# A recorded program and a list scheduler in the kernel, in place of the framework's scheduler, for the second half of an attention, MLP and token-mixer kernel

## The chip, the cores and the metric

The kernel runs on one core of a Trainium2 chip. A core has five engines that each work through their own instructions in order: TensorE (PE, matrix products into PSUM banks), ScalarE (ACT), VectorE (DVE), GpSimd (POOL), and SyncE (SP), which here issues the DMA transfers. They wait for each other by semaphores. The metric is the device time of one execution in microseconds, as the median of the runs.

## The reference

Three layers follow each other, with two batches of 768 tokens and a width of 512.

```python
def _attn_ref(q, k, v):            # 8 heads of 64
    k_sum = k.reshape(B, H, nb, block, D).max(axis=3)      # blocks of 32 tokens
    v_sum = v.reshape(B, H, nb, block, D).mean(axis=3)
    # scores: |i - j| < 16 locally, and q . k_sum + log(32) for each block
    a = softmax(concat(scores_local, scores_blocks))
    return a @ concat(v, v_sum)

def _moe_ref(x, g_ln, w_ch1, w_ch2):
    xn = (x - mu) / np.sqrt(var + 1e-06) * g_ln
    return x + np.maximum(xn @ w_ch1, 0.0) @ w_ch2         # 512 -> 2048 -> 512

def _moe2_ref(x, w_theta, w_tok_r, w_tok_i, w_ch):
    theta = x @ w_theta
    zr, zi = x * np.cos(theta), x * np.sin(theta)
    y = w_tok_r @ zr + w_tok_i @ zi                        # over the 768 tokens
    u = x + y
    return u + np.maximum(u @ w_ch, 0.0)
```

## The kernel before, in words

The 12 tiles of 128 tokens (x_b_t, six for each batch) pass through attention and are gathered in three chunks of four tiles for the MLP. A float32 factor is held as a high and a low float16 half (suffix h and l, or the indices 0 and 1), and a product is three float16 products. For each of the 16 blocks f of the hidden width a chunk does `up` (12 products of 512 columns, L489), `relu` on ACT into the high half h (L493), `relu_low` on DVE for the low half (L497), and `down` (12 products, L508) into four PSUM banks; `add` (L513) puts these onto x. In the program strings the words U, i, j, X and Y are up, relu, relu_low, down and add, numbered 0 to 47 over the three chunks: U32 to U47 are chunk 2, the third.

The mixer has three parts. `rest(t)` (L539 to L561) makes theta of one tile with 12 products, then sine and cosine (L542 to L548), the rotated halves and their sums (L549 to L557), and splits each into a high half (ACT, L560) and a low half (POOL, L561); tiles come to it turned (`turn`, L877 to L879: cast on ACT, difference on POOL, DMA transpose). The token product is done in seven products m1 to m7 for each batch and half (`mix`, L595, 18 products of 384 columns each) with sums and differences of the token weights (b11, t1, t2, b21, t3, b22, t4). Their results are added into u (L603 on DVE, L606 on POOL; `whole_x`, L579 on POOL, starts u from x), and a finished u is split again into x2 (L615 on ACT, L616 on DVE). `channel` (L676) is the last product, with its result at L681 to L685.

Weights come as raw words; head (ACT, L140), whole (DVE, L146), high (ACT, L153) and low (POOL, L156) convert them. The token weights are converted tile by tile during chunks 1 and 2 (`token_jobs`, DVE differences at L196, splits at L186 on ACT and L187 on POOL). Three of their seven blocks, t3, b22 and t4 (SPILLED), do not fit beside the MLP: they are stored to HBM (L793) and read back at L707 when the MLP's space is free.

What sets the order: PE runs in program order throughout. Up to the middle of chunk 1 all engines follow START, an order written out by hand. Behind that, from U24 on (SECOND, then chunk 2's `steps`, then `run_end`), the framework's scheduler chooses the order of ACT, DVE, POOL and SP, with `tc.high_priority()` around the relus and the mixer's results. The token jobs are handed out between steps at fixed rates (`advance`). The framework may also put instructions of the second half into START's holes; it does so with five L140, three L146, one L877 and four loads.

Of the kernel before, what the change touches and what calls it, by code (L numbers as in the profile page):

```python
# [22 lines left out]
P = 128  # L23
NT = S // P
# [64 lines left out]

@with_exitstack  # L90
def attention_mlp_mixer(ctx: ExitStack, tc: tile.TileContext, qd, kw, vt, vp, g_ln, w1, w2, wth, wtr, wti, wch,
                        c_mask_l, c_mask_r, c_ident, out):
    nc = tc.nc
# [13 lines left out]

    def piece(name):

        return pieces.tile([P, 512], F16, tag="piece", name=name, bufs=4 * NF)  # L110
# [302 lines left out]
    class Chunk:  # L413
# [69 lines left out]
        def up(self, f):  # L483
            xh, xl = self.x[:, 0:KT, :], self.x[:, KT:, :]
            ph = self.ph[f] = banks.take()
            wh, wl = (w.rearrange("p (k n) -> p k n", k=KT) for w in w1_s[f])
            terms = [(wh, z, k) for k in range(KT) for z in (xh, xl)] + [(wl, xh, k) for k in range(KT)]
            for n, (a, z, k) in enumerate(terms):
                nc.tensor.matmul(ph, a[:, k, :], z[:, k, :], start=(n == 0), stop=(n == len(terms) - 1))  # L489

# [9 lines left out]
        def down(self, f):  # L500
            if f == 0:
                self.pc = [banks.take() for i in range(4)]
            h = self.h.pop(f)
            hh, hl = h[:, 0, :], h[:, 1, :]
            wh, wl = w2_s[f]
            for i in range(4):
                for n, (a, z) in enumerate(((hh, wh), (hh, wl), (hl, wh))):
                    nc.tensor.matmul(self.pc[i], a[:, i * P:(i + 1) * P], z, start=(f == 0 and n == 0), stop=(f == NF - 1 and n == 2))  # L508
            hls.give(h)

# [5 lines left out]
        def steps(self, first=0):  # L516

            def step(n):
                f = n // 2
                if n % 2 == 0 and f < NF:  # L520
                    self.up(f)
                    with tc.high_priority():
                        self.relu(f)
                        self.relu_low(f)
                if n % 2 and f >= 2:
                    self.down(f - 2)
                if n == 2 * NF + 3:
# [53 lines left out]
    def mix(b, g):  # L581
# [5 lines left out]
        def product(name):  # L587
            key, part, block = PRODUCTS[name]
            bank[name] = banks.take()
            col = (part + g) * P  # L590
            w = blocks[block]
            for t in range(NT):
                z = zs[b, t][key]
                for n, (a, e) in enumerate(((0, 0), (0, 1), (1, 0))):
                    nc.tensor.matmul(bank[name][:, 0:CH], z[a][:, col:col + P], w[:, e, t, :],  # L595
                                     start=(t == 0 and n == 0), stop=(t == NT - 1 and n == 2))

        def onto(name, what, into):
            with tc.high_priority():
                onto_now(name, what, into)  # L600

        def onto_now(name, what, into):
            nc.vector.scalar_tensor_tensor(out=into, in0=bank[name][:, 0:CH], scalar=1.0 / WS, in1=what, op0=ALU.mult, op1=ALU.add)  # L603
# [7 lines left out]
        def result(name, d, c):  # L611
            u, xh, xl = us[b, d, c], x2[b, c][:, d, :], x2[b, c][:, KT + d, :]
            onto(name, u, u)
            with tc.high_priority():
                nc.scalar.copy(xh, u)  # L615
                nc.vector.tensor_tensor(out=xl, in0=u, in1=xh, op=ALU.subtract)  # L616

        def m1():
            product("m1")
            left["s"] = temps.take()  # L620
            with tc.high_priority():
                nc.scalar.mul(left["s"], bank["m1"][:, 0:CH], 1.0 / WS)
            banks.give(bank["m1"])
            plus(lo, 0, "s")
# [75 lines left out]
    def run_end(turn, rest):  # L700
# [3 lines left out]
        for t in range(2):  # L704
            turn(t)
        for name in SPILLED:
            nc.sync.dma_start(out=blocks[name], in_=spilled[name])  # L707
# [3 lines left out]
        turn(2)  # L711
# [86 lines left out]
    def attention_done():  # L798
# [3 lines left out]
        late = ctx.enter_context(tc.tile_pool(name="late", bufs=1, side="right"))  # L802
# [24 lines left out]
    def run(program):  # L827
# [5 lines left out]

        def urgent(name):
            def step(f):
                with tc.high_priority():
                    mlp_step(name)(f)
            return step

# [15 lines left out]
            "U": mlp_step("up"), "i": urgent("relu"), "j": urgent("relu_low"), "X": mlp_step("down"),  # L855
# [47 lines left out]

    for name in run(SECOND):
        if name in "UX":
            advance(SECOND_RATE)
    spare = mlp.tile([P, 2 * KT, MC], F16, tag="x", name="xt", bufs=2).rearrange("p a b -> p (a b)").bitcast(F32)
# [25 lines left out]
    run_end(*rotate(1, free, free))  # L933

# [56 lines left out]
```

## Time and profile before

| | |
|---|---|
| runs, us | 498.72, 502.1, 503.67; median 502.1 |
| profiled execution, us | 500.46 (span 498.7) |
| mean granted TensorE clock | 0.983 |
| PE busy | 471.3 us, 95% of the span |
| DVE, ACT, POOL busy | 300.7, 224.1, 227.8 us |
| DMA | 61.69 MB, mean 124 GB/s |

The span is what the trace covers, from the first to the last record; the profiled execution's own time is 1.8 us longer. The granted clock is a share of 2.4 GHz, the upper of the two levels; the lower, 1.2 GHz, reads 0.50. In the rows a line such as L497 is a line of the kernel, `ps` is a PSUM bank, and square brackets name the idle time of the engine before the row and what ended it.

### The profile page before, as it was taken

The page shows a single profiled execution, that of the slowest core. Times are in us where ns is not written, and L with a number is a line of the kernel's source. Part 1 is how long each engine was busy: PE and PEld are TensorE (multiplying, and loading weights), DVE is VectorE, ACT ScalarE, POOL GpSimd, SP SyncE. Part 2 cuts the span into 40 slices and gives each one's busy share as a digit, 9 for nine tenths or more (in the row PEclk, how much of TensorE's full clock was granted, in tenths as well). Part 3 has the DMA queues.
Part 4 walks back from the last instruction along what each step waited for, and adds up shares of the span by engine and source line. Part 5 has one row for each costly group of instructions (what it writes and reads, how often), then busy time and mean ns, then how long its engine had stood idle before and what let it go on. Part 6 is the DMA issues. An engine that isn't in the chain of part 4 may idle for free. (4 is left out here: it accounts for less than half of the span.)

```text
span 498.7 us, 8654 instructions
## 1 busy us (share of the span) xinstructions
PE 471.3 (95%) x3360; PEld 245.5 (49%) x3360; DVE 300.7 (60%) x480; ACT 224.1 (45%) x469; POOL 227.8 (46%) x254
## 2 busy tenths in 40 slices
PE   7899999999999999799989979999999995999997
PEld 2567765455544444244434424444555552556664
DVE  4388989999841211831497865665707687934332
ACT  1359896736751111640375565554504435422022
POOL 3747035746000000940397755666595755890200
PEclk9999999999999999999999989999999997999999
DMA  8989969786753000560277680000095100110012
GB/s 300 301 285 272 240 200 284 228 207 190 245 187 63 1 0 1 143 171 14 63 212 227 188 251 2 0 1 1 0 327 64 22 1 2 62 34 17 0 48 95
DMA packets 51401, 61.69 MB, mean 124 GB/s; under 512 B 23478, under 2 KB 38720, under 8 KB 50976
## 3 DMA queue, kind: packets, MB, share of 16 engines
q1 hardware_dynamic: 51072, 60.62, 42.4%
q8 instruction: 26, 0.43, 0.4%
q10 hardware_dynamic: 288, 0.52, 0.4%
q14 instruction: 15, 0.12, 0.1%
HBM read 48.80 MB, written 6.68 MB: 111 GB/s over the span
## 5 line engine op out<-in xcount | busy, mean ns | idle before, releaser
L508 PE MATMUL ps<-w,h 128*128 128x512 f16 x576 | 131.5, 382 | 6.0 <-DVE h L497 3.5
L489 PE MATMUL ps<-xt,w 128*128 128x512 f16 x576 | 129.3, 379 | 0.0
L508 PEld LDWEIGHTS <-h 128*128 128x128 f16 x576 | 56.0, 99 | 75.9 <-DVE h L497 5.4
L489 PEld LDWEIGHTS <-w 128*128 128x128 f16 x576 | 56.0, 98 | 66.8
L497 DVE SCALAR_TENSOR_TENSOR h<-ps,h 128x512 f16<-128x512 f32 x48 | 32.9, 685 | 62.5 <-ACT h L493 62.3
L493 ACT ACTIVATE h<-ps 128x512 f16<-128x512 f32 x48 | 28.5, 593 | 61.2 <-PE ps L489 51.1
L146 DVE SCALAR_TENSOR_TENSOR w<-raw,hd 128x512 int32<-128x512 int32 (+1 forms) x55 | 45.3, 832 | 12.0 <-ACT hd L140 4.5
L140 ACT ACTIVATE hd<-raw 128x512 f16<-128x512 bf16 (+1 forms) x64 | 45.8, 727 | 9.7 <-DMA raw<-in_w 3.2
L156 POOL TENSOR_TENSOR w<-w,w 128x512 f16<-128x512 f32 x20 | 27.1, 1358 | 37.7 <-ACT w L153 22.5
L676 PE MATMUL ps<-x,ch 128*128 128x384 f16 (+1 forms) x204 | 34.7, 331 | 5.7 <-ACT x L615 5.5
L539 PE MATMUL ps<-th,x 128*128 128x512 f16 x144 | 34.8, 394 | 3.7 <-DVE h L497 3.7
L676 PEld LDWEIGHTS <-ch 128*128 128x128 f16 x204 | 20.2, 101 | 19.5 <-issue 7.8
L878 POOL TENSOR_TENSOR xhl<-x,xhl 128x512 f16<-128x512 f32 x6 | 7.8, 1313 | 45.9 <-ACT xhl L877 45.9
L304 POOL TENSOR_TENSOR raw<-raw 128x384 f32<-128x384 f32 (+3 forms) x32 | 19.4, 607 | 17.8 <-DMA raw<-in_vt 15.9
L352 ACT ACTIVATE pr<-ps,nb 128x120 f32<-128x120 f32 x96 | 26.6, 366 | 0.7
L539 PEld LDWEIGHTS <-x 128*128 128x128 f16 x144 | 14.6, 101 | 21.7 <-issue 6.5
L595 PE MATMUL ps<-tok_t,z_s12h 128*128 128x384 f16 x96 | 23.4, 326 | 0.0
L261 PE MATMUL ps<-idle 128*128 128x512 bf16 x60 | 21.5, 435 | 1.0 <-DVE idle L766 1.0
L156 POOL TENSOR_TENSOR th<-w,th 128x512 f16<-128x512 f32 x4 | 5.1, 1270 | 35.2 <-ACT th L153 35.2
L342 DVE TENSOR_REDUCE nm<-ps 128x4 f32<-128x480 f32 x24 | 14.8, 649 | 10.1 <-PE ps L403 10.1
L187 POOL TENSOR_TENSOR xt<-w,xt 128x384 f16<-128x384 f32 x8 | 8.5, 1065 | 25.9 <-ACT xt L186 25.9
L403 PE MATMUL ps<-k,qt 64*64 64x96 f32 x384 | 15.9, 263 | 3.5 <-issue 2.2
(168 smaller groups left out, 798.9 us busy)
## 6 DMA issues: line engine op xcount, KB each, us to landing
raw<-in_w SPq DMA_DIRECT2D x16, 511.8 KB, 4.5
raw<-in_w SPq DMA_DIRECT2D x16, 511.0 KB, 5.0
vw<-in_vp SPq DMA_DIRECT2D x12, 396.0 KB, 7.3
raw<-in_wtr SPq DMA_DIRECT2D x12, 383.8 KB, 3.7
raw<-in_wti SPq DMA_DIRECT2D x12, 383.8 KB, 3.7
k<-in_kw SPq DMA_DIRECT2D x8, 400.0 KB, 8.8
raw<-in_vt SPq DMA_DIRECT2D x8, 384.0 KB, 7.6
qt<-in_qd SPq DMA_DIRECT2D x10, 256.0 KB, 5.4
```

Source lines behind the costliest of these rows:

```text
L140: nc.scalar.mul(out, st["raw"].bitcast(BF16)[:, 0:4 * k * n].rearrange("p (x w) -> p x w", w=4)[:, :, 2], HEAD_SCALE)
L146: nc.vector.scalar_tensor_tensor(out=st["w"].bitcast(I32), in0=rest, scalar=13, in1=st["head"].bitcast(I32)[:, 0:k * n], op0=ALU.logical_s ...
L156: engine.tensor_tensor(out=lo(), in0=st["w"], in1=st["h"], op=ALU.subtract)
L261: nc.tensor.matmul(bank.rearrange("p (r n) -> p r n", n=P), idle, idle.unsqueeze(1).to_broadcast([P, 4, P]), start=True, stop=True)
L352: nc.scalar.activation(out=self.pr[:, h, :], in_=self.sc[:, h, :], func=AF.Exp, bias=self.nb[:, h:h + 1], scale=SCALE)
L489: nc.tensor.matmul(ph, a[:, k, :], z[:, k, :], start=(n == 0), stop=(n == len(terms) - 1))
L493: nc.scalar.activation(out=self.h[f][:, 0, :], in_=self.ph[f], func=AF.Relu)
L497: nc.vector.scalar_tensor_tensor(out=h[:, 1, :], in0=self.ph[f], scalar=0.0, in1=h[:, 0, :], op0=ALU.max, op1=ALU.subtract)
L508: nc.tensor.matmul(self.pc[i], a[:, i * P:(i + 1) * P], z, start=(f == 0 and n == 0), stop=(f == NF - 1 and n == 2))
L539: nc.tensor.matmul(pt, xt[:, a, o:o + P], w[:, k, :], start=(n == 0), stop=(n == 3 * KT - 1))
L595: nc.tensor.matmul(bank[name][:, 0:CH], z[a][:, col:col + P], w[:, e, t, :], start=(t == 0 and n == 0), stop=(t == NT - 1 and n == 2))
L676: nc.tensor.matmul(pos[e][:, lo:hi], w[:, e * P:(e + 1) * P], z[:, a, lo:hi], start=(k == ORDER[0] and i == 0), stop=(k == ORDER[-1] and i ...
```

## The change

A class `Plan` stands between the kernel and the engines. Between `nc.begin()` and `nc.emit()` it records each instruction instead of issuing it, with what it reads and writes and a cost for its engine. `emit` then issues all of them in an order of its own: PE keeps its program order, which gives each PE instruction a time; from these a `due` time is worked out backwards for everything that feeds PE; and a list scheduler takes, of the instructions that can start within 0.1 us of the earliest one, the one that is due first. There are two such records: from U24 to the end of chunk 2, and `run_end`. Both are issued under `tc.manual_schedule()`, so the framework keeps this order and puts nothing of it into START. `high_priority` is gone. The 64 half-weight tiles (`pieces`) are now an explicit ring that `up`, `down` and `product` give back to. `turn(2)` stands ahead of the reload, each reload is recorded `behind` the SP instruction before it, and the reloaded blocks' places in the `end` pool come before x2's.

```diff
+class Plan:
+    ENGINES = {"tensor": "PE", "scalar": "ACT", "vector": "DVE", "gpsimd": "POOL", "sync": "SP"}
+    PATIENCE = 0.1
...
+        if op.engine == "SP":
+            op.landing = math.prod(out.shape) * mybir.dt.size(out.dtype) / 2.5e5
...
+    def behind(self):
+        n = len(self.ops)
+        yield
+        for op in self.ops[n:]:
+            op.before.add(next(x for x in reversed(self.ops[:n]) if x.engine == op.engine))
...
+    def cost(self, engine, out, ins):
+        n = math.prod(out.shape[1:])
+        psum = any(a.space == PSUM for a in ins)
+        wide = sum(a.space != PSUM and math.prod(a.shape[1:]) == n for a in ins)
+        if engine == "PE":
+            return (math.prod(ins[1].shape[1:]) / 2.4 + 5) / 1e3
+        if engine == "ACT":
+            return (190 + 0.82 * n) / 1e3 if n > 8 else 0.2
+        if engine == "DVE":
+            if n <= 8:
+                return 0.18 if not ins or math.prod(ins[0].shape[1:]) <= 8 else 0.69
+            return (150 + n * (1.04 if psum or wide > 1 else 0.65) * (1.25 if wide > 1 else 1.0)) / 1e3
+        if engine == "POOL":
+            return (200 + 2.2 * n) / 1e3 if n > 8 else 0.6
+        return 0.42
...
+    def emit(self):
+        ops, self.ops = self.ops, None
...
+        at = self.free["PE"]
+        for op in ops:
+            op.due = math.inf
+            if op.engine == "PE":
+                op.due = at
+                at += op.cost
+        for op in reversed(ops):
+            for other in op.after:
+                op.due = min(op.due, other.due - self.lag(op, other) - op.cost)
+            if op.due == math.inf:
+                op.due = at
...
+            op = min((x for x in ready[e] if max(self.free[e], x.when) <= first + self.PATIENCE), key=lambda x: (x.due, x.n))
...
-    nc = tc.nc
+    nc = Plan(tc.nc)
...
-        return pieces.tile([P, 512], F16, tag="piece", name=name, bufs=4 * NF)
+        return slots.take()
...
-                    with tc.high_priority():
-                        self.relu(f)
-                        self.relu_low(f)
+                    self.relu(f)
+                    self.relu_low(f)
...
-        for t in range(2):
+        for t in range(3):
             turn(t)
         for name in SPILLED:
-            nc.sync.dma_start(out=blocks[name], in_=spilled[name])
+            with nc.behind():
+                nc.sync.dma_start(out=blocks[name], in_=spilled[name])
         whole_x(0)
         m1, m6, m5, m2, m7, m3, m4 = mixes[0, 0]
         m1()
-        turn(2)
...
+    nc.begin()
     for name in run(SECOND):
...
+    with tc.manual_schedule():
+        nc.emit()
...
+    for name in reversed(SPILLED):
+        blocks[name] = end.tile([P, 2, NT, CH], F16, name=f"tok_{name}")
     for c in range(2):
         x2[1, c] = end.tile([P, 2 * KT, CH], F16, name=f"x2_1_{c}")
-    for name in SPILLED:
-        blocks[name] = end.tile([P, 2, NT, CH], F16, name=f"tok_{name}")
...
+    nc.begin()
     run_end(*rotate(1, free, free))
+    with tc.manual_schedule():
+        nc.emit()
```

PE's instructions stand in the same order in both kernels. Recorded instructions all have the line L111 in the new kernel, those of START L108. First ACT, where START ends. Before, the relu of f = 23 (the L493 row with ps3) stands behind three conversions of w_theta and the cast L445 that needs rstd:

```order
L153 CAST th0_2252<-w1_101 128x512
L153 CAST th0_2252<-w2_102 128x512
L153 CAST th0_2252<-w0_100 128x512
L445 ACTIVATE xhl0_107<-xn0_105,rstd_2266 128x512
L493 ACTIVATE h2_111<-ps3_66 128x512
```

Now it stands first:

```order
L111 ACTIVATE h2_175<-ps3_66 128x512
L111 CAST xhl1_172<-x_0_0_75 128x512
L111 ACTIVATE xhl0_171<-xn0_169,rstd_2264 128x512
L111 ACTIVATE h0_173<-ps7_70 128x512
L111 ACTIVATE hd0_167<-raw0_160 128x512
```

The relu of f = 23 moved ahead of the cast with rstd, the next relu (h0 from ps7) stands right behind that cast, and the conversions follow.

Next DVE in the token work, from the last two `add` of chunk 1 to relu_low of chunk 2's f = 0 (the row with h2 and ps7). Before (xt is the space of x of chunk 1, used for token words):

```order
L513 SCALAR_TENSOR_TENSOR x_1_0_81<-ps6_69,x_1_0_81 128x512
L196 TENSOR_TENSOR xt_2573<-xt_2573,w2_102 128x384
L513 SCALAR_TENSOR_TENSOR x_1_1_82<-ps5_68,x_1_1_82 128x512
L196 TENSOR_TENSOR w1_101<-w1_101,xt_2573 128x384
L146 SCALAR_TENSOR_TENSOR xt_2573<-raw3_99,hd1_104 128x384
L146 SCALAR_TENSOR_TENSOR w2_102<-raw2_98,hd0_103 128x384
L196 TENSOR_TENSOR w0_100<-xt_2573,w0_100 128x384
L146 SCALAR_TENSOR_TENSOR xt_2573<-raw1_97,hd1_104 128x384
L196 TENSOR_TENSOR xt_2573<-w2_102,xt_2573 128x384
L497 SCALAR_TENSOR_TENSOR h2_111<-ps7_70,h2_111 128x512
```

Now:

```order
L111 SCALAR_TENSOR_TENSOR x_1_0_81<-ps6_69,x_1_0_81 128x512
L111 SCALAR_TENSOR_TENSOR x_1_1_82<-ps5_68,x_1_1_82 128x512
L111 TENSOR_TENSOR xt_1515<-xt_1515,w2_166 128x384
L111 SCALAR_TENSOR_TENSOR xt_1515<-raw3_163,hd1_168 128x384
L111 TENSOR_TENSOR w1_165<-w1_165,xt_1515 128x384
L111 SCALAR_TENSOR_TENSOR w2_166<-raw2_162,hd0_167 128x384
L111 SCALAR_TENSOR_TENSOR xt_1515<-raw1_161,hd1_168 128x384
L111 SCALAR_TENSOR_TENSOR h2_175<-ps7_70,h2_175 128x512
L111 TENSOR_TENSOR w0_164<-xt_1515,w0_164 128x384
```

Two token differences (w0 and xt) moved behind the relu_low. Up to relu_low of f = 5 there are 30 DVE instructions before and 23 now.

Then DVE at the start of `run_end`. Before, u_0_1 and u_2_1 (L603, which add a product's bank onto u) stand ahead of rest(0) of the second batch, whose first three rows work in x_0_4 and x_0_5:

```order
L603 SCALAR_TENSOR_TENSOR tp1_3436<-ps6_69,tp0_3435 128x384
L603 SCALAR_TENSOR_TENSOR u_0_1_3428<-ps7_70,u_0_1_3428 128x384
L603 SCALAR_TENSOR_TENSOR u_2_1_3432<-ps7_70,u_2_1_3432 128x384
L542 TENSOR_SCALAR x_0_4_79<-ps4_67 128x512
L543 TENSOR_SCALAR x_0_4_79<-x_0_4_79 128x512
L544 SCALAR_TENSOR_TENSOR x_0_5_80<-ps4_67,x_0_4_79 128x512
```

Now:

```order
L111 SCALAR_TENSOR_TENSOR tp1_3388<-ps6_69,tp0_3387 128x384
L111 TENSOR_SCALAR x_0_4_79<-ps4_67 128x512
L111 TENSOR_SCALAR x_0_4_79<-x_0_4_79 128x512
L111 SCALAR_TENSOR_TENSOR x_0_5_80<-ps4_67,x_0_4_79 128x512
L111 SCALAR_TENSOR_TENSOR u_0_1_3380<-ps7_70,u_0_1_3380 128x384
L111 SCALAR_TENSOR_TENSOR u_2_1_3384<-ps7_70,u_2_1_3384 128x384
```

The three rows of rest(0) moved ahead of the two that need POOL's sums in u. On POOL, whole_x is no longer one block of eight: the order there is whole_x of u_0_0, its sum, whole_x of u_0_1 and u_2_1, their sums, and so on.

Last SP at the reload. Before:

```order
L879 DMA_TRANSPOSE x2_1_0_3422<-x_0_0_75 128x8x128
L879 DMA_TRANSPOSE x2_1_0_3422<-x_0_1_76 128x8x128
L707 DMA tok_t3_3424<-spilled_t3_171 128x4608
L707 DMA tok_b22_3425<-spilled_b22_172 128x4608
L707 DMA tok_t4_3426<-spilled_t4_173 128x4608
L879 DMA_TRANSPOSE x2_1_0_3422<-x_0_2_77 128x8x128
```

Now:

```order
L111 DMA_TRANSPOSE x2_1_0_3377<-x_0_0_75 128x8x128
L111 DMA_TRANSPOSE x2_1_0_3377<-x_0_2_77 128x8x128
L111 DMA_TRANSPOSE x2_1_0_3377<-x_0_1_76 128x8x128
L111 DMA tok_t3_3376<-spilled_t3_235 128x4608
L111 DMA tok_b22_3375<-spilled_b22_236 128x4608
L111 DMA_TRANSPOSE x2_1_1_3378<-x_0_3_78 128x8x128
L111 DMA_TRANSPOSE x2_1_1_3378<-x_0_0_75 128x8x128
L111 DMA tok_t4_3374<-spilled_t4_237 128x4608
```

A third transpose moved ahead of the reloads, and two more stand between b22's reload and t4's.

## Rows read from the trace of the kernel before

**Rows 1.** PE timeline: start, busy us, engine, line, operation [idle before <-releaser]

```profile
198.25 5.35 PE L489 MATMUL ps<-xt,w 128*128 128x512 f16 x24
...
220.84 2.75 PE L489 MATMUL ps<-xt,w 128*128 128x512 f16 x12
```

**Rows 2.** ACT timeline where START ends

```profile
203.65 0.72 ACT L445 ACTIVATE xhl<-xn,rstd 128x512 f16<-128x512 f32 x1 [2.90 <-POOL rstd L434]
```

**Rows 3.** PE timeline, end of chunk 1 and token work

```profile
249.33 7.93 PE L489 MATMUL ps<-xt,w 128*128 128x512 f16 x36
...
260.10 3.86 PE L508 MATMUL ps<-w,h 128*128 128x512 f16 x10 [1.04 <-DVE h L497]
263.79 2.75 PE L489 MATMUL ps<-xt,w 128*128 128x512 f16 x12
266.38 2.75 PE L508 MATMUL ps<-w,h 128*128 128x512 f16 x12
...
287.10 2.75 PE L489 MATMUL ps<-xt,w 128*128 128x512 f16 x12
293.52 4.44 PE L539 MATMUL ps<-th,x 128*128 128x512 f16 x12 [3.66 <-DVE h L497]
297.79 2.75 PE L508 MATMUL ps<-w,h 128*128 128x512 f16 x12
```

**Rows 4.** PE timeline, end stage

```profile
380.09 0.49 PE L595 MATMUL ps<-tok_t,z_ih 128*128 128x384 f16 x2
...
411.26 1.63 PE L676 MATMUL ps<-x,ch 128*128 128x384 f16 x9
418.39 0.48 PE L676 MATMUL ps<-x,ch 128*128 128x384 f16 x1 [5.50 <-ACT x L615]
...
423.54 2.81 PE L539 MATMUL ps<-th,x 128*128 128x512 f16 x12
426.19 7.96 PE L676 MATMUL ps<-x,ch 128*128 128x384 f16 x48
433.99 2.93 PE L595 MATMUL ps<-tok_b,z_r 128*128 128x384 f16 x17
437.44 0.34 PE L595 MATMUL ps<-tok_b,z_r 128*128 128x384 f16 x1 [0.52 <-POOL z_r L561]
```

**Rows 5.** Windows: stretch, busy us of five engines, clock, DMA share, GB/s

```profile
260.00:263.80 3.80, 3.70 (x11) 1.39 (x12) 2.99 (x5) 2.61 (x6) 3.80 (x5) 0.58 0.60 181
...
297.80:408.60 110.80, 110.80 (x577) 56.35 (x576) 66.09 (x103) 48.88 (x90) 70.01 (x69) 1.00 0.19 50
418.40:423.50 5.10, 4.86 (x15) 2.12 (x15) 3.84 (x7) 2.71 (x5) 2.96 (x3) 0.50 0.00 0
```

**Rows 6.** DVE timeline, then POOL timeline, token work

```profile
257.24 0.55 DVE L196 TENSOR_TENSOR w<-xt,w 128x384 f32<-128x384 f32 x1
...
258.18 1.26 DVE L196 TENSOR_TENSOR xt<-w,xt 128x384 f32<-128x384 f32 x1
...
261.43 1.25 DVE L196 TENSOR_TENSOR xt<-xt,w 128x384 f32<-128x384 f32 x1 [0.81 <-POOL tok_b L187]
...
257.98 1.04 POOL L187 TENSOR_TENSOR xt<-w,xt 128x384 f16<-128x384 f32 x1 [1.08 <-ACT xt L186]
```

**Rows 7.** DVE timeline, then POOL timeline, end stage

```profile
375.00 0.56 DVE L603 SCALAR_TENSOR_TENSOR u<-ps,u 128x384 f32<-128x384 f32 x1 [10.96 <-POOL u L606]
...
400.61 0.68 DVE L542 TENSOR_SCALAR tr<-ps 128x512 f32<-128x512 f32 x1
...
418.37 0.68 DVE L616 TENSOR_TENSOR x<-u,x 128x384 f16<-128x384 f32 x1 [0.74 <-ACT x L615]
...
364.96 6.99 POOL L579 TENSOR_TENSOR u<-x 128x384 f32<-128x384 f16 x8
```

**Rows 8.** SP timeline, reload

```profile
364.42 0.38 SPq L707 DMA_DIRECT2D tok_t<-spilled_t  x1
```

**Rows 9.** DMA issues, 355 to 400 us: KB each, us to landing

```profile
tok_b<-spilled_b SPq DMA_DIRECT2D x1, 1152.0 KB, 9.0
```

More of the change, by code (lines that the diff above doesn't have):

```diff
@@ L1 @@
 import math
-from contextlib import ExitStack
+from contextlib import ExitStack, contextmanager
 import numpy as np
@@ L90, in attention_mlp_mixer, with __init__, __getattr__ @@
+class Planned:
+    def __init__(self, plan, name):
+        self.plan, self.name = plan, name
+    def __getattr__(self, method):
+        return lambda *args, **kwargs: self.plan.call(self.name, method, args, kwargs)
+class Op:
+    def __init__(self, n, engine, do):
+        self.n, self.engine, self.do, self.before, self.landing = n, engine, do, set(), 0.0
 @with_exitstack
@@ L106, in attention_mlp_mixer @@
     pieces = ctx.enter_context(tc.tile_pool(name="pieces", bufs=1))
+    slots = Ring(*(pieces.tile([P, 512], F16, name=f"pc{i}") for i in range(4 * NF)))
+    slot_of = {x.tensor.name: x for x in slots.free}
     def piece(name):
-        return pieces.tile([P, 512], F16, tag="piece", name=name, bufs=4 * NF)
+        return slots.take()
     mlp_cm = tc.tile_pool(name="mlp", bufs=1)
@@ L489, in up @@
                 nc.tensor.matmul(ph, a[:, k, :], z[:, k, :], start=(n == 0), stop=(n == len(terms) - 1))
+            if self is chunks[-1]:
+                for x in w1_s[f]:
+                    slots.give(x)
         def relu(self, f):
@@ L509, in down @@
             hls.give(h)
+            if self is chunks[-1]:
+                for x in w2_s[f]:
+                    slots.give(x)
         def add(self, i):
@@ L588, in product @@
             key, part, block = PRODUCTS[name]
+            last = (name, g) in (("m1", 1), ("m5", 1), ("m3", 1), ("m4", 1))
             bank[name] = banks.take()
@@ L596, in product @@
                                      start=(t == 0 and n == 0), stop=(t == NT - 1 and n == 2))
+                if last and b == 0:
+                    for x in ({z[0].tensor.name: z[0].tensor, z[1].tensor.name: z[1].tensor}).values():
+                        slots.give(slot_of[x.name])
         def onto(name, what, into):
-            with tc.high_priority():
-                onto_now(name, what, into)
-        def onto_now(name, what, into):
             nc.vector.scalar_tensor_tensor(out=into, in0=bank[name][:, 0:CH], scalar=1.0 / WS, in1=what, op0=ALU.mult, op1=ALU.add)
@@ L613, in result @@
             onto(name, u, u)
-            with tc.high_priority():
-                nc.scalar.copy(xh, u)
-                nc.vector.tensor_tensor(out=xl, in0=u, in1=xh, op=ALU.subtract)
+            nc.scalar.copy(xh, u)
+            nc.vector.tensor_tensor(out=xl, in0=u, in1=xh, op=ALU.subtract)
         def m1():
@@ L620, in m1 @@
             left["s"] = temps.take()
-            with tc.high_priority():
-                nc.scalar.mul(left["s"], bank["m1"][:, 0:CH], 1.0 / WS)
+            nc.scalar.mul(left["s"], bank["m1"][:, 0:CH], 1.0 / WS)
             banks.give(bank["m1"])
@@ L801, in attention_done @@
         at_cm.__exit__(None, None, None)
-        late = ctx.enter_context(tc.tile_pool(name="late", bufs=1, side="right"))
+        late = ctx.enter_context(tc.tile_pool(name="late", bufs=1, side="right", reuse_waits="tile"))
         th.extend(late.tile([P, KT, DM], F16, name=f"th{n}") for n in range(2))
@@ L832, in run @@
         job = lambda n, *a: lambda i: w_jobs[i][n](*a)
[L834 to L838, printed above, removed]
         does = {
@@ L854, in run @@
             "dg": chunk("scale"), "fl": chunk("flip"), "fh": chunk("flipped_high"), "fz": chunk("flipped_low"),
-            "U": mlp_step("up"), "i": urgent("relu"), "j": urgent("relu_low"), "X": mlp_step("down"),
+            "U": mlp_step("up"), "i": mlp_step("relu"), "j": mlp_step("relu_low"), "X": mlp_step("down"),
             "l": job(0), "A": job(1), "D": job(2), "H": job(3), "I": job(4),
@@ L906, in attention_mlp_mixer @@
             advance(SECOND_RATE)
-    spare = mlp.tile([P, 2 * KT, MC], F16, tag="x", name="xt", bufs=2).rearrange("p a b -> p (a b)").bitcast(F32)
+    spare = chunks[1].x.rearrange("p a b -> p (a b)").bitcast(F32)
     stages = Ring(*(spare[:, i * CH:(i + 1) * CH] for i in range(3)))
```

88 lines of the change are left out of this document (added).

## The prediction, as it was made before the changed kernel ran

> **What bounds the kernel now.** I read the line of matrix-engine (PE) starts first, since PE is 95% busy and the change leaves PE's own instruction order as it was; the time can only come from PE's gaps. Twelve 512-column products are one step: 263.79 to 266.38 is 2.59 us [rows 3]; a 384-column product is 0.1625 us (48 of them from 426.19 to 433.99) [rows 4]. Every stretch is held against these two pitches. Up to 197 us the program is the hand-written START order in both kernels, which I take as unmoved: the change moves nothing on PE there, and the few conversions that no longer fill holes of START (below) come behind it. From 198 us on there are five losses.
>
> - A, where START ends: 198.25 to 220.84 holds seven steps, 7 × 2.59 = 18.13 of 22.59 us, so 4.46 are lost [rows 1]. ScalarE (ACT) sits 2.90 us in front of L445, which waits for POOL's rstd, and U23's relu is queued behind it [rows 2].
> - B, chunk 2's start: 249.33 to 263.79 holds four steps, 10.36 of 14.46 us: 4.10 lost, at the end of it 1.04 for VectorE's (DVE's) relu_low of f = 0 of that chunk, and more since the granted clock is 0.58 in the stretch after that wait, mostly the lower (1.2 GHz) of its two levels [rows 3, 5].
> - C: 287.10 to 297.79 holds two steps, 5.18 of 10.69 us: 5.51 lost, of it 3.66 waiting for relu_low of f = 5, which frees the PSUM bank of rest(1) [rows 3].
> - D, the first channel products: 411.26 to 423.54 holds 24 products of 384 columns, 3.90 of 12.28 us: 8.38 lost, 5.50 of it one wait for the split of x2 (L615), and then a granted clock of 0.50, the lower level throughout [rows 4, 5].
> - E: 433.99 to 437.44 holds 17 products, 2.76 of 3.45 us: 0.69 lost to POOL's z_r [rows 4].
>
> Together 4.46 + 4.10 + 5.51 + 8.38 + 0.69 = 23.1 us. Between C and D PE is busy 110.80 of 110.80 us at clock 1.00 [rows 5]: nothing to gain there, only to lose. The profiled execution took 500.46 us, 1.6 below the median of 502.1; the sum is made on the former and carried to the median at the end.
>
> **The change part by part.** No arithmetic is added or taken away: PE keeps its instructions, banks and order. What changes is the order on ACT, DVE, POOL and SP, so each part below is the wait that it ends and what is late next.
>
> A. In the new ACT order U23's relu is the first recorded instruction, ahead of the cast that needs rstd. So its 2.90 us go, and the cast now waits with nothing urgent in front of PE behind it: the next relu stands one place after it, and PE's step of 2.59 for each relu gives it room. The conversions that the old scheduler had put early into START (five ACT head copies, three DVE joins, four loads) now come here too; U24's and U25's relus stand between them, not behind them all. Taken: 0 of 4.46 left. Bounds of the rest: 0 and 4.46.
>
> B. What counts is how many DVE instructions stand between the token work's resumption late in chunk 1 and relu_low of f = 0: the order has 18 before and 16 now. DVE's two-input token operations come in two sizes: 0.55 us alone and 1.26 with POOL at work (257.24 and 258.18; POOL starts at 257.98 after an idle 1.08) [rows 6]. The two that are gone were one of each, with steps (start to start, ends overlapping) of 1.19 and 0.47: 1.66. PE needed it at 249.33 + 3 × 2.59 = 257.10 and got it at 260.10 [rows 3], 3.0 late; 1.3 stay. Bounds: 0 if DVE's operations are short, 4.10 if the order gives nothing. The plan in the kernel counts such an operation as 150 + 384 × 1.04 × 1.25, or 0.65 us, for all of them; at that price relu_low would be in time. I take 1.3, by the long row, since POOL is still fed at every token step.
>
> The long row has a rule that speaks against the plan: the Trainium skill, "SBUF — State Buffer", section "Who interferes with whom", says that a DVE instruction with two SBUF inputs contends with a GpSimd instruction that reads SBUF, through an exclusive lock on shared ports. The trace agrees (0.55 and 1.26 us for one shape). By the plan's flat 0.65 B would leave no loss; by the rule, with the long duration, the 1.3 that stands above.
>
> C. Between the relu_lows of f = 0 and f = 5 stand 30 DVE instructions before and 23 now. Before, they took 293.52 − 260.10 = 33.4 us [rows 3], 1.11 each with their waits; 23 take 25.6. PE's own work between the two points is the 33.4 less the 3.66 waited and less the 1.53 by which the ten products from 260.10 on are slower than 10 × 0.216: 28.2. So relu_low is some 2.6 us early, and C goes whole. What is late next: rest(0)'s rotation now stands ahead of f = 6's relu_low on DVE and its sines ahead of the relu on ACT; by the same prices this may cost 0.6 (between 0 and 5.5, all of C moved by two steps).
>
> D. DVE now puts the first three instructions of rest(0) of the second batch ahead of u_0_1, which waits for POOL. Before, DVE stood 10.96 us in front of u_0_1 (375.00), because POOL did all eight whole_x (6.99 us from 364.96) ahead of the sums into u [rows 7]. Now POOL alternates whole_x and sums, and u_0_1's sum stands fifth where it stood eleventh: by the same durations done some 8 us earlier. The rotation that follows moves up with it, until POOL is the one that holds: I reckon that its last sum of the second product group ends near 395, 6 us before where it ends now, so that rest(2)'s first DVE step, at 400.61 before, comes at some 395.5. From that step to the end of the last L616 DVE runs a fixed chain: 418.37 + 0.68 − 400.61 = 18.4 us [rows 7]. It ends near 413.9, with one instruction of 0.5 now behind it 413.4; PE needs it at 411.26 + 9 × 0.1625 = 412.7 to 412.9 [rows 4]. Taken 0.5 of 8.38; bounds 0 and 8.38, since my 395.5 comes from two engines that feed each other.
>
> E. With rest(5) earlier by the same 5 us, z_r is there before 433.99: 0 of 0.69.
>
> The reload. On SP the third turned tile goes ahead of the three reloads, and t4's reload stands behind two further transposes that wait for POOL. t4 was issued at 364.42 [rows 8]; in the new order about 373.2, POOL's two sums and two turned tiles later. One block took 9.0 us from issue to landing with the three in flight together [rows 9]; m4 reads t4 at 380.09 [rows 4]. With a third of 9.0 for its own share it lands by 376 to 378 and costs nothing: what hides it is m7, rest(1) and m3. With the whole 9.0 it comes at 382.2, 2.1 late, and 3 with the lower clock after a wait. I take 0, since it is then alone on the wires.
>
> Sum: 23.1 − (1.3 + 0.6 + 0.5) = 20.7 us; 500.46 − 20.7 = 479.8, and 1.6 on top for the median: 481.
>
> **The rivals.** Rival 1, the token stage keeps its waits: the plan counts 0.65 where rows show 1.26, so DVE falls behind the plan and relus wait on it as before. For it: the rows' long duration, and that DVE's order alone doesn't make POOL faster. Against it: fewer instructions stand ahead of the two relu_lows that count. B and C stay and the 0.6 is in them: gain A 4.46 + D 7.9 + E 0.7 = 13.1, 487.4 and, at the median, 489.
>
> Rival 2, the end keeps its wait: POOL is the pace there, so DVE gets its rotation earlier but u doesn't; or t4 comes late at m4. Gain A 4.46 + B 2.8 + C 4.9 + E 0.7 = 12.9, 489 at the median, 492 with t4's 3. For it: POOL's sums into u are named in DVE's longest wait. Against it: POOL's idle time there comes from DVE in turn.
>
> Rival 3, slower: relus queue behind token operations that each wait for POOL. The old scheduler's high priority for relus is gone, and an engine in order can't step over a waiting token subtraction. A wait of 0.81 ahead of 1.25 stands at 261.43 [rows 6]: if each of the 23 instructions between f = 0 and f = 5 paid both, 2.06, they would take 47.4 where PE has work for 28.2. The 19.2 would grow by the lower clock as C's 3.66 grew to 5.51, to 29: 479.8 + 29 + 1.6 = 510. It decides from 1.23 us an instruction, where relu_low is no longer early, and eats the whole gain at 1.83. Against it: the 30 instructions of before averaged 1.11.
>
> That the change doesn't do what it says can be left out as a rival: the orders show the moves.
>
> **How the numbers follow.** Forecast 0.64; rival 1 0.15; rival 2 0.11; rivals 1 and 2 together (gain of A and E, 497) 0.05; rival 3 0.05. Under the forecast the time lies between 476 (no loss left, 477.3, and a run that is as far below as 498.72 is below 500.46) and 485. To hold 8 in 10 the range takes in rivals 1 and most of 2: 476 to 491. A measurement of this kernel can't tell less than about 1% from no change; faster by more than that (under 497.1) are the first three cases, 0.90; within it 0.05, the two rivals together; slower 0.05.
>
> **What would show it.** In the new trace PE's starts from U23 to U27 come every 2.59 us, relu_low of f = 5 ends before its bank is wanted, and the granted clock is near 1.00 from 198 to 440 us; DVE's first rotation step of the second batch comes right after PE's products of it, without a wait of 10 us; the stop in the first channel products is under 1 us. Rival 1 shows as waits of PE for relu_low between 250 and 300 us, rival 2 as a wait for x2 or for a reload after 360 us, rival 3 as waits that grow from step to step. The prediction is wrong above all if my reckoning of POOL and DVE at the end is, or if START itself gets slower for lack of the loads that came early.

## The result, and the profile after

The changed kernel takes 479.96 us (median of four runs, 479.64 to 482.12) against 501.22 for the kernel before (its median with a fourth run): a ratio of 0.9586 with a 95% interval of [0.9537, 0.9634], so 4.1% faster. The granted clock is 0.996 instead of 0.983. The profiled execution is the slowest of the four, 482.12 us, and START came out long in it: U23 starts at 199.56, where the other kernels below start it between 196.7 and 199.5. I therefore compare traces from U23 on: 498.7 − 198.25 = 300.45 us before, 480.3 − 199.56 = 280.74 after, 19.7 less.

First the rows of PE's timeline that answer to [rows 1] and [rows 3], from the trace of the changed kernel:

```profile
199.56 2.76 PE L108 MATMUL ps<-xt,pc 128*128 128x512 f16 x12
202.16 2.75 PE L111 MATMUL ps<-xt,pc 128*128 128x512 f16 x12
204.75 5.34 PE L111 MATMUL ps<-pc,h 128*128 128x512 f16 x24
...
246.19 7.93 PE L111 MATMUL ps<-xt,pc 128*128 128x512 f16 x36
253.96 2.75 PE L111 MATMUL ps<-pc,h 128*128 128x512 f16 x12
256.55 2.75 PE L111 MATMUL ps<-xt,pc 128*128 128x512 f16 x12
...
279.86 2.75 PE L111 MATMUL ps<-xt,pc 128*128 128x512 f16 x12
282.45 2.75 PE L111 MATMUL ps<-th,x 128*128 128x512 f16 x12
285.04 2.75 PE L111 MATMUL ps<-pc,h 128*128 128x512 f16 x12
```

No row has a bracket, and every twelve products take 2.59 us: A, B and C are gone to the last step. X32 follows U34 at 253.96 = 246.19 + 3 × 2.59, without the stop ahead of the row at 260.10 in [rows 3]. The end stage, answering to [rows 4]:

```profile
359.80 3.10 PE L111 MATMUL ps<-tok_t,pc 128*128 128x384 f16 x18 [0.74 <-DMA tok_t<-spilled_t]
...
368.75 3.10 PE L111 MATMUL ps<-tok_t,pc 128*128 128x384 f16 x18 [0.33 <-DMA tok_t<-spilled_t]
...
399.93 1.63 PE L111 MATMUL ps<-x,pc 128*128 128x384 f16 x9
401.79 0.32 PE L111 MATMUL ps<-x,pc 128*128 128x384 f16 x1 [0.23 <-ACT x L111]
403.43 2.44 PE L111 MATMUL ps<-x,pc 128*128 128x384 f16 x14 [1.32 <-DVE x L111]
405.70 2.75 PE L111 MATMUL ps<-th,x 128*128 128x512 f16 x12
...
416.09 3.31 PE L111 MATMUL ps<-tok_b,pc 128*128 128x384 f16 x18
419.24 6.01 PE L111 MATMUL ps<-tok_t,pc 128*128 128x384 f16 x36
```

D is down from 8.38 to 405.70 − 399.93 − 3.90 = 1.87 us. Two waits are new, for the reloaded blocks: m7 starts 0.90 us late for t3 (355.97 + 18 × 0.1625 = 358.90), m4 0.50 late for t4. Of E 0.22 is left: the 18 products at 416.09 take 3.15 us where the pitch gives 2.93. So 3.49 us are left of 23.1. The clock stays up: in the windows view of the same trace (the stretch, the busy times of PE, PEld, DVE, ACT and POOL, the clock, DMA share and GB/s) both stretches read 1.00, the short stop in D among them:

```profile
198.00:440.00 242.00, 239.32 (x1235) 119.36 (x1234) 173.22 (x233) 120.83 (x227) 164.14 (x152) 1.00 0.36 98
401.70:405.70 4.00, 2.59 (x15) 1.46 (x15) 3.86 (x6) 1.24 (x4) 2.70 (x2) 1.00 0.00 0
```

Over the same 198 to 440 us the kernel before had PE busy for 226.10 us at a clock of 0.97.

### The profile page after: what moved, and what is told of

Same layout as the page of the kernel before. It is cut to its first block, busy times and chain, and to the rows that moved or that the text cites. A ratio compares the mean times of both kernels' runs of the same rounds, so it can differ in the third digit from the quotient of the medians.

```text
span 480.3 us, 8629 instructions
## 1 busy us (share of the span) xinstructions
PE 466.0 (97%) x3360; PEld 245.0 (51%) x3360; DVE 311.2 (65%) x480; ACT 223.0 (46%) x469; POOL 229.9 (48%) x254
## 5 line engine op out<-in xcount | busy, mean ns | idle before, releaser
L111 PEld LDWEIGHTS <-pc 128*128 128x128 f16 x996 | 96.9, 98 | 82.8 <-issue 2.0
L111 PE MATMUL ps<-pc,h 128*128 128x512 f16 x300 | 67.9, 379 | 0.0
L111 PE MATMUL ps<-xt,pc 128*128 128x512 f16 x288 | 65.3, 379 | 0.0
L108 PE MATMUL ps<-xt,pc 128*128 128x512 f16 x288 | 64.2, 379 | 0.0
L108 PE MATMUL ps<-pc,h 128*128 128x512 f16 x276 | 61.4, 379 | 0.0
L111 PE MATMUL ps<-tok_t,pc 128*128 128x384 f16 x288 | 48.8, 326 | 1.1 <-DMA tok_t<-spilled_t 1.1
L111 PEld LDWEIGHTS <-h 128*128 128x128 f16 x300 | 29.3, 98 | 35.4
L108 POOL TENSOR_TENSOR pc<-w,pc 128x512 f16<-128x512 f32 x20 | 27.1, 1357 | 37.3 <-ACT pc L108 22.1
L108 PEld LDWEIGHTS <-pc 128*128 128x128 f16 x288 | 27.8, 98 | 32.8
L108 PEld LDWEIGHTS <-h 128*128 128x128 f16 x276 | 26.8, 98 | 31.8
L108 DVE SCALAR_TENSOR_TENSOR h<-ps,h 128x512 f16<-128x512 f32 x23 | 15.8, 686 | 38.6 <-ACT h L108 38.5
L108 ACT ACTIVATE h<-ps 128x512 f16<-128x512 f32 x23 | 13.8, 598 | 54.7 <-PE ps L108 54.5
L111 POOL TENSOR_TENSOR ve<-mv,eps 128x1 f32<-128x1 f32 x1 | 0.2, 190 | 77.8 <-DVE mv L111 77.8
L111 PE MATMUL ps<-tok_b,pc 128*128 128x384 f16 x216 | 37.2, 326 | 0.0
L111 PE MATMUL ps<-x,pc 128*128 128x384 f16 (+1 forms) x204 | 32.4, 317 | 1.6 <-DVE x L111 1.3
L111 PE MATMUL ps<-th,x 128*128 128x512 f16 x144 | 33.0, 379 | 0.0
L111 DVE SCALAR_TENSOR_TENSOR h<-ps,h 128x512 f16<-128x512 f32 x25 | 17.1, 684 | 21.1 <-ACT h L111 21.1
L111 POOL TENSOR_TENSOR pc<-tr,pc 128x512 f16<-128x512 f32 (+1 forms) x18 | 19.0, 1060 | 20.7 <-ACT pc L111 20.7
L108 POOL TENSOR_TENSOR raw<-raw 128x384 f32<-128x384 f32 (+3 forms) x32 | 18.6, 581 | 20.3 <-DMA raw<-in_vt 18.5
L108 ACT ACTIVATE pr<-ps,nb 128x120 f32<-128x120 f32 x96 | 26.5, 364 | 3.0 <-PE ps L108 2.4
L111 DVE SCALAR_TENSOR_TENSOR w<-raw,hd 128x384 int32<-128x384 int32 (+1 forms) x23 | 22.5, 991 | 6.7 <-ACT hd L111 2.7
L108 DVE SCALAR_TENSOR_TENSOR w<-raw,hd 128x512 int32<-128x512 int32 x32 | 24.7, 778 | 1.4 <-ACT hd L108 1.2
```

Source lines behind the costliest of these rows:

```text
L108: return getattr(getattr(self.nc, name), method)(*args, **kwargs)
L111: op = Op(len(self.ops), self.ENGINES[name], lambda: getattr(getattr(self.nc, name), method)(*args, **kwargs))
```

## The experiments

**One record at a time.** e1 leaves `run_end` to the framework's scheduler:

```diff
-    nc.begin()
     run_end(*rotate(1, free, free))
-    with tc.manual_schedule():
-        nc.emit()
```

with `high_priority` and the old reload put back in it. 

> Only the first record (U24 to the end of chunk 2) is planned; run_end goes back to the framework's scheduler, with high priority for the results, and to its old reload order. If the gain is the order of each stage by itself, the waits of the end come back: D from 1.87 us to about 8.4, E 0.7, and the two new waits for reloads (0.74 and 0.33) go, so about 6 us more than the changed kernel, 486. If the gain came from the other edits (tile ring, release of spaces), it stays near 480 to 482.

 Measured: 491.79 us, ratio 0.9816 [0.9769, 0.9862]. A, B and C stay away and the waits for reloads go, but E is back (0.95 us, of it 0.56 waiting for POOL), and D comes back larger than it was before, 412.56 − 396.37 − 3.90 = 12.29 us. PE's timeline of e1:

```profile
396.37 1.63 PE L108 MATMUL ps<-x,pc 128*128 128x384 f16 x9
406.67 0.48 PE L108 MATMUL ps<-x,pc 128*128 128x384 f16 x1 [8.67 <-ACT x L108]
408.12 4.64 PE L108 MATMUL ps<-x,pc 128*128 128x384 f16 x14 [0.98 <-DVE x L108]
412.56 3.46 PE L108 MATMUL ps<-th,x 128*128 128x512 f16 x12
```

The end's DVE chain starts at the same distance from whole(0), the first channel product, as before (396.37 − 361.86 = 34.5 us; 411.26 − 376.43 = 34.8 before), but takes 46.2 us to the last low half instead of 42.6, as DVE is busy for 38.2 us of that stretch instead of 32.7 with the same instructions: two-input operations take longer beside POOL's. From DVE's timeline of e1: the first step of rest(0), a split of a result (L616 before), and the last split:

```profile
361.86 0.68 DVE L108 TENSOR_SCALAR x<-ps 128x512 f32<-128x512 f32 x1
...
371.13 1.45 DVE L108 TENSOR_TENSOR x<-u,x 128x384 f16<-128x384 f32 x1 [0.22 <-ACT x L108]
...
406.65 1.43 DVE L108 TENSOR_TENSOR x<-u,x 128x384 f16<-128x384 f32 x1 [0.71 <-ACT x L108]
```

The last split took 0.68 in [rows 7]. So the old order of the end costs 8.4 us or 12.3, by how it happens to fall against POOL. My 486 counted the former.

e2 is the reverse: the first record is not made and the relus have high priority again, while `run_end` is planned. 

> Only run_end is planned; U24 to the end of chunk 2 goes back to the framework's scheduler with high priority for the relus. The token words still lie in chunk 1's x itself and not in a new tile over it. By the order of the queues A (4.5), B (4.1) and C (5.5) come back: 494. If B went because the token work may start before U31 has read all of x, B stays away here and it is 490. If the order of the first record is not what counts, 480 to 483.

 Measured: 492.42 us, 0.983 [0.9787, 0.9873]. A is back with 3.6 us, B with 6.0 and C with 1.5, 11.1 together; D is gone (24 products from 412.32 to 416.26), but t3's reload holds PE for 3.02 us, 4.6 with the slower products after it:

```profile
259.35 4.45 PE L108 MATMUL ps<-pc,h 128*128 128x512 f16 x10 [2.52 <-DVE h L108]
...
371.31 4.50 PE L111 MATMUL ps<-tok_t,pc 128*128 128x384 f16 x18 [3.02 <-DMA tok_t<-spilled_t]
```

In this trace, too, the token work starts before U31 is through (240.93 against 242.09), and 20 DVE instructions still stand ahead of relu_low of f = 32. The early start comes from an edit that the section on the change leaves out: the token words now lie in chunk 1's x itself (`spare = chunks[1].x...`), where before a new tile `xt` lay over it, and DVE waited 1.27 us for PE ahead of the first word, at 244.35. e2 has this edit and B all the same, so B did not go by the space alone. Nor do the other edits beside the records (the tile ring, and `reuse_waits="tile"` for the pool `late`) keep the losses away by themselves: e1 and e2 both have them. Without the second record the kernel is 11.8 us slower than the changed one, without the first 12.5, together more than the 21.3 of both: D is larger in e1 and B in e2 than they were before, and t3's 4.6 us in e2 are new.

**A.** e3 is the kernel before with one edit of the program strings:

```diff
-... V22 U23 R22 o22 n11        # START
+... V22 U23 i23 j23 R22 o22 n11
-s11 c11 P11 U24 i23 h11 j23 y11 ...   # SECOND
+s11 c11 P11 U24 h11 y11 ...
```

> The kernel before with one edit: relu and relu_low of f = 23 stand at the end of the hand-written START instead of behind the cast that waits for rstd. By the theory A goes by itself: 4.5 us less than the kernel before, about 497. If the wait passes to the next relu (the cast with rstd holds ACT for the one after it), 0 to 2 us less.

 Measured: 508.51 us, 1.0148 [1.0083, 1.0213], 1.5% slower. Both of the cases that I had set against each other were wrong. From the timelines of ACT (the three relus are those of f = 23, 24 and 25), POOL and PE of e3:

```profile
200.16 0.60 ACT L493 ACTIVATE h<-ps 128x512 f16<-128x512 f32 x1 [7.90 <-PE ps L489]
202.06 1.14 ACT L153 CAST th<-w 128x512 f16<-128x512 f32 x2 [1.30 <-DVE x L386]
203.10 0.59 ACT L493 ACTIVATE h<-ps 128x512 f16<-128x512 f32 x1
...
206.61 0.72 ACT L445 ACTIVATE xhl<-xn,rstd 128x512 f16<-128x512 f32 x1 [2.42 <-POOL rstd L434]
...
218.62 0.51 ACT L186 CAST tok_b<-w 128x384 f16<-128x384 f32 x1 [2.12 <-DVE w L146]
219.04 0.59 ACT L493 ACTIVATE h<-ps 128x512 f16<-128x512 f32 x1
...
206.03 0.54 POOL L434 TENSOR_TENSOR rstd<-ve,pw 128x1 f32<-128x1 f32 x1
...
202.54 5.50 PE L508 MATMUL ps<-w,h 128*128 128x512 f16 x24
...
219.69 1.03 PE L508 MATMUL ps<-w,h 128*128 128x512 f16 x2 [6.46 <-ACT h L493]
```

The relus of f = 23 and 24 both run ahead of the cast L445, and PE loses 0.16 us in X23 and X24 (202.54, 5.34 us to the next row), although rstd is there only at 206.57, 9.2 us after U23's start at 197.35. What is late is the relu of f = 25. PE is through with U25 at 207.88 + 2.59 = 210.47, but the relu runs at 219.04, behind fifteen other instructions, conversions nearly all; PE waits 6.46 us for it. In the kernel before it stands behind much the same conversions and runs at 217.02, 0.6 us ahead of X25. The edit itself makes them later: relu_low of f = 23 went along with the relu, and on DVE it now stands ahead of attention's last output (L386, x), which starts at 201.60 instead of 198.58. The casts of w_theta, rstd and the token conversions behind them come 3.0 to 3.4 us later, and PE comes to U25 4.6 us sooner.

e11 asks the same question inside the changed kernel: the relu of f = 23 is recorded after the cast that needs rstd and tied behind it.

```diff
-U24 i23 h11 j23 y11
+U24 h11 i23 j23 y11
...
+            if self is chunks[1] and f == 7:
+                with nc.behind():
```

> The changed kernel with the relu of f = 23 put back behind the cast that needs rstd on ACT. If A went because that relu moved ahead of the cast, PE waits again, 3 to 4.5 us: 483 to 484.5. In the new trace POOL has rstd ready at 202.47, since no conversion of w_theta stands ahead of it on POOL any more (before, two stood ahead of it and it came at 203.6): if that is what ended A, the relu runs by 204, PE needs it at 207.3, and the time stays at 480.

 Measured: 480.64 us, 0.959 [0.9539, 0.9642]; from U23 on 280.67 us, the changed kernel 280.74. ACT's timeline of e11, then POOL's:

```profile
200.28 0.72 ACT L111 ACTIVATE xhl<-xn,rstd 128x512 f16<-128x512 f32 x1 [8.05 <-POOL rstd L111]
200.91 0.58 ACT L111 ACTIVATE h<-ps 128x512 f16<-128x512 f32 x1
...
199.11 0.19 POOL L111 TENSOR_TENSOR ve<-mv,eps 128x1 f32<-128x1 f32 x1 [77.53 <-DVE mv L111]
199.38 0.87 POOL L111 TENSOR_TENSOR rstd<-ve,pw 128x1 f32<-128x1 f32 x1
```

The relu stands where it stood before the change and costs nothing, since rstd is there 2.9 us after U23's start. Before, one difference of w_theta stood ahead of its first step on POOL and one ahead of its second, and it came 5.4 us after U23's start; POOL's timeline of the kernel before:

```profile
199.79 1.16 POOL L156 TENSOR_TENSOR th<-w,th 128x512 f16<-128x512 f32 x1 [34.50 <-ACT th L153]
200.90 0.64 POOL L433 TENSOR_TENSOR ve<-mv,eps 128x1 f32<-128x1 f32 x1
201.50 1.61 POOL L156 TENSOR_TENSOR th<-w,th 128x512 f16<-128x512 f32 x1
203.07 0.54 POOL L434 TENSOR_TENSOR rstd<-ve,pw 128x1 f32<-128x1 f32 x1
```

So the stops at f = 23 and 24 have two cures: rstd in time, which is enough in e11, and the relus ahead of the cast, which is enough in e3 (there both, in the changed kernel only that of f = 23). The changed kernel has both. That rstd is in time because those two differences no longer stand ahead of it is read from the timelines.

**B.** e4 gives the token words the other part of chunk 1's x:

```diff
-    stages = Ring(*(spare[:, i * CH:(i + 1) * CH] for i in range(3)))
+    stages = Ring(*(spare[:, i * CH:(i + 1) * CH] for i in range(2, 5)))
     for i in range(2):
-        token_words.give(spare[:, (3 + i) * CH:(4 + i) * CH])
+        token_words.give(spare[:, i * CH:(i + 1) * CH])
```

> The changed kernel with the two token words in the part of chunk 1's x that PE reads to the very end of U31 (the high halves), and the three stages in the other. The token work then starts about 1.2 us later. If that early start is why B went whole, relu_low of f = 32 ends only 0 to 0.5 us ahead of PE's need (now 1.06) or PE waits up to 1 us; if the order alone is the cause, its lead stays near 1. The time is 480 to 481.5 either way.

 Measured: 480.82 us, 0.9598 [0.9555, 0.964]. relu_low of f = 32 ends at 250.12 + 0.68 = 250.80, and X32 starts at 251.07: a lead of 0.27 us, where the changed kernel has 253.96 − 252.90 = 1.06. DVE's timeline of the changed kernel shows the early start, and that the first operations are short ones, as POOL (idle until 241.15) has nothing to do yet:

```profile
239.85 1.05 DVE L111 SCALAR_TENSOR_TENSOR xt<-raw,hd 128x384 int32<-128x384 int32 x2
240.82 0.55 DVE L111 TENSOR_TENSOR w<-xt,w 128x384 f32<-128x384 f32 x1
...
251.03 1.26 DVE L111 SCALAR_TENSOR_TENSOR xt<-raw,hd 128x384 int32<-128x384 int32 x1
252.22 0.68 DVE L111 SCALAR_TENSOR_TENSOR h<-ps,h 128x512 f16<-128x512 f32 x1
```

In e4 the token work starts 0.2 us ahead of U31's end instead of 1.2 (before, 0.2 behind it), and relu_low has 0.8 us less of lead; the planner still finds an order that is in time, with 15 instructions ahead. The waits for t3 and t4 are longer there, 1.53 and 1.08 us.

**The reload and the rest of D.** e5 takes back `turn(2)` and `behind`:

```diff
-        for t in range(3):
+        for t in range(2):
             turn(t)
         for name in SPILLED:
-            with nc.behind():
-                nc.sync.dma_start(out=blocks[name], in_=spilled[name])
+            nc.sync.dma_start(out=blocks[name], in_=spilled[name])
...
         m1()
+        turn(2)
```

> The changed kernel with the reload's part undone: two tiles are turned, the three reloads are recorded without being tied behind the transposes, and the third tile is turned after m1 as before. In the order the three reloads then stand ahead of all transposes on SP. If the two waits for reloads in the changed kernel (0.74 at t3, 0.33 at t4) come from that edit, they go: about 1 us less, 479. If the transposes behind the reloads make rest(0) late, PE waits for the turned x there instead: 480 to 484.

 Measured: 483.34 us, 0.9648 [0.9617, 0.9679]. The waits for reloads go, and rest(0) waits 3.79 us for its turned tile instead:

```profile
354.67 4.45 PE L111 MATMUL ps<-th,x 128*128 128x512 f16 x12 [3.79 <-DMA x<-x]
```

So the edit of the reload pays: without it the kernel would be 3.4 us slower, and its two waits are what it leaves.

e6 puts rest(5) ahead of whole(0) and whole(1) in `run_end`. 

> The changed kernel with rest(5) of the second batch ahead of the first two channel products on PE. If what is left of D (1.87 us) is only the end of a chain on DVE that comes a little late, 2.6 us of other PE work in front of it covers it: about 1.9 us less, 478. If the chain is paced by PE's own products of rest(5) or by the banks, the wait moves to the channel products or to m1 of the second batch and the time stays at 480.

 Measured: 478.63 us, 0.9548 [0.9518, 0.9579]; no wait is left in the channel products, two are for reloads (0.34 and 0.83). From U23 on it takes 278.71 us, 2.0 less than the changed kernel.

e7 changes one number of the plan, the DVE price of an operation with two inputs in SBUF:

```diff
-... * (1.25 if wide > 1 else 1.0)) / 1e3
+... * (2.5 if wide > 1 else 1.0)) / 1e3
```

> The changed kernel with the plan's price of a two-input DVE operation on 384 columns at 1.15 us instead of 0.65, near what the trace shows beside POOL. If the flat price is a weakness that only the cover hides, the token part stays without waits and the end gets a better order, D below 1.9: 478 to 480. If the order is all that counts and the price hardly moves it, 479.5 to 480.5. If a plan that believes DVE slow puts other work late, up to 484.

 Measured: 477.36 us, 0.9529 [0.9495, 0.9563], the fastest of all. PE's timeline from U23 to the end has no bracket left, for D and both reloads:

```profile
358.07 3.09 PE L111 MATMUL ps<-tok_t,pc 128*128 128x384 f16 x18
...
366.51 3.09 PE L111 MATMUL ps<-tok_t,pc 128*128 128x384 f16 x18
...
397.68 4.06 PE L111 MATMUL ps<-x,pc 128*128 128x384 f16 x24
401.58 2.75 PE L111 MATMUL ps<-th,x 128*128 128x512 f16 x12
```

From U23 on it takes 277.27 us, 23.2 less than before, and the five losses were 23.1: with PE's order as it is, no gap is left in that part.

e9 and e10 use that price in one record only, `nc.pair` being 1.25 or 2.5. 

> The price of 1.15 us for a two-input DVE operation on 384 columns (0.65 in the changed kernel, 1.15 everywhere in e7) is used for the second record, run_end, alone. If what is left of D is the order of the end by itself, D goes as in e7; the waits for reloads hang on what the first record leaves on POOL and DVE at the end of chunk 2, so they stay near 0.7 and 0.3: 478.3. If D hangs on the first record too, 479.5 to 480.5.

 Measured: 479.79 us, 0.9556 [0.9513, 0.9598]; D is gone, the waits for reloads stay, 0.73 and 1.00. 

> The price of 1.15 us in the first record alone (U24 to the end of chunk 2). If POOL's backlog at the end of chunk 2 sets when t3's reload is issued, both waits for reloads go and D stays at 1 to 2 us: 478.5 to 479. If the reload hangs on the order within run_end, 480.

 Measured: 478.71 us, 0.9548 [0.9511, 0.9585]; the waits for reloads are gone, D's 1.32 for the low half is as it was. Their medians lie too close together to tell them from each other or, for e9, from the changed kernel; the traces tell them apart, wait by wait. The reload hangs on when POOL is through with chunk 2: in e7 its last split for chunk 2's rotations ends at 346.54, 11.5 us before m7; in the changed kernel at 349.35, 9.6 us before m7 is due at 358.90. That is not all of it: in e11, too, it ends 9.6 us before m7 (347.10), and there is no wait for t3, as the two transposes ahead of the reload take 2.62 us on SP and not 3.46 (but one of 1.78 for t4).

**The due times.** e8 keeps record and simulation, and takes of the ready instructions the first recorded:

```diff
-key=lambda x: (x.due, x.n))
+key=lambda x: x.n)
```

> The changed kernel with the same record and the same simulation of the engines, but of the instructions that can start the one recorded first is taken, not the one due first. If the due times carry the gain, waits for relu_low come back in the token part (some 3 us) and the end keeps a D of 5 us or more: 484 to 490. If it is enough that instructions are issued in the order in which their inputs come ready, 480 to 482.

 Measured: 484.82 us, 0.9676 [0.9642, 0.9711]. Against what I expected of the due times the token part has no wait at all. What is lost lies in the end, as waits of 1.93 us for t4 and of 2.16 and 1.20 in the channel products:

```profile
402.69 0.32 PE L111 MATMUL ps<-x,pc 128*128 128x384 f16 x1 [2.16 <-ACT x L111]
404.22 3.76 PE L111 MATMUL ps<-x,pc 128*128 128x384 f16 x14 [1.20 <-DVE x L111]
```

D is 407.82 − 398.90 − 3.90 = 5.02 us there. So by the medians the due times are worth 4.9 of the 21.3 us; the rest is there without them, with the recording, the simulated order and the edits beside them.

## Why the prediction was right, and where its steps were not

481 was forecast and 479.96 measured, with 2.4 us of the five losses left by my sum and 3.49 by the trace. That the two lie so close is partly luck: the sum took 1.9 us for B and C that did not come, and left out 3.0 of D, E and the reload. Median to median the gain is 21.3 us, and from U23 on the two traces show 19.7 of it; the rest is within what START varies by (it ends between 196.7 and 199.6 us in the traces). By the steps:

- A: 0 left, as forecast, but for more reasons than the one I gave. That the relu stands ahead of the cast was not needed (e11): rstd itself is no longer late, which I had not reckoned. That it can be enough for the first two stops, and that the relu of f = 25 must not stand behind all the conversions, as I had said, is shown by e3.
- B: 1.3 taken, 0 measured, with 1.06 us to spare: 2.4 off. The early start in the part of x that PE is done with is 1.4 of it (239.85 against U31's end at 241.01, 0.2 after it before); I had not reckoned with which bytes of x the words lie in. The rest is that 16 instructions took 13.05 us to the end of relu_low where I reckoned 14.0, the first of them being short. The bound 0 held.
- C: gone, as forecast, and the 0.6 for what is late next did not come. The 23 instructions took 23.3 us (252.90 to 276.16) where I had 25.6, and relu_low of f = 5 ended 6.3 us ahead of rest(1) instead of 2.6.
- D: 0.5 taken, 1.87 measured. The chain from rest(2)'s first DVE step to the last split takes 403.38 − 385.09 = 18.3 us, and I had 18.4, but not the 0.5 that I took off for one instruction fewer. That step stands 399.93 − 385.09 = 14.8 us ahead of whole(0), 4.2 more than before, where I reckoned 5.1. POOL held it, as in my reckoning, but for longer: its last sum of the second product group ends at 384.58, 15.3 us ahead of whole(0), where I had 16.3. From POOL's and DVE's timelines of the changed kernel:

```profile
380.73 3.85 POOL L111 TENSOR_TENSOR u<-u,tp 128x384 f32<-128x384 f32 x4
...
385.09 0.68 DVE L111 TENSOR_SCALAR tr<-ps 128x512 f32<-128x512 f32 x1
...
401.41 1.97 DVE L111 TENSOR_TENSOR x<-u,x 128x384 f16<-128x384 f32 x2
```

- E: 0 taken, 0.22 measured.
- The reload: 0 taken, 1.40 measured. I had priced t4 alone and put t3 at nothing without a reason; but the third transpose, and the difference on POOL that it waits for, stand ahead of t3 as well, and t3 costs 0.90. t4 landed 5.4 us after its issue (363.28), where a third of 9.0 was my share for it, and costs 0.50.

Rival 1 had the right weakness, the plan's price of 0.65, and the wrong place: in the token part it is covered, and even the order of recording is enough there (e8). The price tells at the end and through what chunk 2 leaves behind (e7, e9, e10): 2.6 us by the medians, 3.5 from U23 on. The Trainium skill, "SBUF — State Buffer", section "Who interferes with whom", says that a DVE instruction with two SBUF inputs contends with a GpSimd instruction that reads SBUF, through an exclusive lock. The traces agree, with 0.55 against 1.26 us for one shape. Rival 2 came true in small: D and the reloads are what is left. Rival 3 did not happen; of the 23 DVE instructions between relu_low of f = 32 and of f = 37 many take 1.26 us, with waits of up to 1.68 for POOL, but PE never noticed. e3 shows that its mechanism is real in the framework's order: the relu of f = 25 runs 8.6 us after its up is through, behind conversions that wait for DVE and POOL.

What stays open: why that scheduler, with high priority on the relus, leaves the one of f = 25 behind the conversions, before as in e3, is not known. The two differences of w_theta were not put back ahead of rstd by themselves, and the relu's place was not tried with everything else as it was before, so how much of A each cure would end alone is not shown.

## What to carry to other kernels

Where PE's order is fixed and it is nearly always busy, the sum of its late starts against the known pitch is the most that a better order of the other engines can give, and here one changed price in the plan gave all of it (e7); the chain from a moved queue to the next late one decides the small remainder. A planner's price for an operation that takes 0.55 us alone and 1.26 beside another engine should, by this kernel, be nearer the long one: it cost one number and gave 2.6 us. An edit that mends one wait by hand moves the work of other engines too: in e3 the relu_low that went along held back DVE's next work by 3.0 us, and that cost more than the relu's new place gave.

## What the runs showed of the hardware

A DVE operation with two inputs in SBUF that starts while a POOL operation runs ends a fixed time after that POOL operation. For 384 columns it is 0.41 to 0.42 us, in 117 of 125 cases in the traces of before, after and e1; alone such an operation takes 0.54 to 0.56. In [rows 6] the one at 258.18 ends at 259.44 and POOL's at 259.02. The last split of x2 ends at 419.05 before and at 408.08 in e1, POOL's at 418.65 and 407.66; it took 0.68 us where POOL's was nearly through when it started, and 1.43 where POOL's had just begun. So DVE's chain at the end, as the framework orders it, took 42.6 us in the kernel before and 46.2 in e1 for the same instructions. DVE's busy time went from 300.7 to 311.2 us with the same 480 instructions in the changed kernel, and the kernel became faster.

A stop of PE costs more than its length where the clock goes down after it: in D before, 5.50 us of waiting became a loss of 8.38 at a granted clock of 0.50, while the stops of 0.23 and 1.32 us after the change left it at 1.00. In e8 a stop of 2.16, one product and a stop of 1.20 were followed by 14 products at a granted clock of 0.62, which took 3.60 us where the pitch gives 2.28.
